# P.V of an attention kernel in eight tiles of the array instead of four, summed in two banks

## The chip, the cores and the metric

The kernel runs on one core of a Trainium2 chip. The metric is the device time of one execution in microseconds; smaller is better. The core's engines work side by side, each on its own queue: TensorE (PE, with its weight loads shown apart as PEld), VectorE (DVE), ScalarE (ACT), GpSimd (POOL) and SyncE (SP, which here only starts DMAs).

## The reference

The input is `x` of 2048 tokens by 512. It is normalised by layer, goes into a softmax attention over 32 heads of 16 dimensions (no mask) and, beside it, into a feed-forward network with a squared ReLU; the attention's result is multiplied by a SiLU gate made of the network's result and added to `x`. All is fp32.

```python
xn = layernorm(x)
q, k, v = split_heads(xn @ wqkv)                # 32 heads, 2048 x 16 each
p = softmax(einsum("bhqd,bhkd->bhqk", q, k) * 16 ** -0.5)
s = merge_heads(einsum("bhqk,bhkd->bhqd", p, v)) @ wo
h = relu(xn @ w1 + b1) ** 2                     # 2048 x 1792
out = x + s * silu(h @ w2 + b2)
```

## The kernel before

Three stages follow each other. The first normalises and transposes `x` and makes keys, queries and values, which go to HBM. The second, nearly all of the time, is 64 turns. The third sums up the last turn and writes the last rows.

A turn is eight of 512 steps. A step `(qd, qc, kb)` takes four heads (`qd`), 512 queries (`qc`) and 128 keys (`kb`). `scores` makes its P transposed, keys on the partitions and queries along the free side, for two heads at a time, in two matmuls on 64 rows of the array each. `exps` takes the exponential of 128 x 1024 numbers on ACT into a tile `P` in SBUF. V has a column of ones beside each head, so that the sums of the softmax come out of the same product.

Three kinds of work of PE share a turn, all in tiles of 64 rows by 128 columns, so that two matmuls in the two row halves can run side by side. The order is a string written out by hand, a letter for a slot:

- `S`: the scores of two heads into one of two PSUM buffers `S` of two banks, from which ACT takes the exponential at once (`scores`, `exps`, L299 and L303).
- `L`: one matmul in each row half for the feed-forward network, or late in the kernel for the output projection (`lin`, L347). They accumulate in the two banks `spare`. `/` ends the first half of such a block: the two halves change banks, behind a small instruction on POOL (`swap`, L373).
- `0`, `1`, `B`: the scores of one head aside (`aside`), by row half 0 into the bank `acc` (`sides[0]`), by row half 1 into the bank `lin` (`sides[1]`), or both. DVE copies the bank into the tile `P` in SBUF (L322), and ACT takes its exponential from there later. Beside a `0` or `1` stands an `L` of the other row half. Five pairs of such scores go this way in an ordinary turn, eleven through `S`.
- `E` ends one block and begins the next.

57 turns use the string `ORDINARY`, the first `FIRST`, four `TWO_PAIRS` and two `SHORT`.

At the end of a turn stands P.V for its eight steps (`values`, L572). V is the stationary side, 128 keys by 32 columns for a head (16 of them the head's values, the next the ones), and each head writes 32 partitions of the bank `acc`: four column tiles with all 128 rows. The products of eight steps accumulate there. Then `finish` takes the bank into the SBUF tile `ou`: in even turns with a copy (L583), in odd ones with an add of the turn before (L586), whose result goes to HBM. The tiny instructions of `see` follow: ACT and DVE each read an element of the last `P`, and DVE one of `sides[1]`. PE is free to write a side again when DVE has read it.

The lines of `fast_path` behind the turns add up the last turn in two halves of the columns (L884), and matmuls (L889) read the result.

Of the kernel before, what the change touches and what calls it, by code (L numbers as in the profile page):

```python
# [28 lines left out]
OP = mybir.AluOpType  # L29
# [18 lines left out]
@with_exitstack  # L48
def mha_ffn_kernel(ctx: ExitStack, tc: tile.TileContext, x, wqkv, wo, bx, w1, b1, w2, b2, out):
    nc = tc.nc  # L50
    x, out = x[0], out[0]
    ctx.enter_context(tc.manual_schedule())
    keep = ctx.enter_context(tc.tile_pool(name="keep", bufs=1))
    dram = ctx.enter_context(tc.tile_pool(name="dram", bufs=1, space=DRAM))

    ident = keep.tile([128, 128], FT, name="ident")
    make_identity(nc, ident)
    nvalid = keep.tile([1, 1], I32, name="nvalid")
    stat = keep.tile([128, 80], FT, name="stat")

    kdram = [[dram.tile([128, 2, 1024], FT, name=f"kd{g}_{h}") for h in range(2)] for g in range(4)]
    qdram = [[dram.tile([128, 2, 512], FT, name=f"qd{g}_{c}") for c in range(NC)] for g in range(4)]
    vdram = dram.tile([NK, 128, VW], FT, name="vd")
    xdram = [dram.tile([128, 2, 4, 512], FT, name=f"xd{c}") for c in range(3)]

    udram = [[dram.tile([2, 2, 16, 4, 512], FT, name=f"ud{g}_{c}") for c in range(NC)] for g in range(4)]
    zdram = [[dram.tile([4, 512], FT, name=f"zd{q}_{c}") for c in range(NC)] for q in range(NQ)]
    gdram = dram.tile([S, D], FT, name="gd")

    with tc.tile_pool(name="sb", bufs=1) as sb, tc.tile_pool(name="ps", bufs=1, space=PSUM) as ps:  # L70
        fast_path(tc, sb, ps, locals())
    general_path(tc, dram, nvalid, ident, vdram, kdram, qdram, gdram, x, wo, out)


def fast_path(tc, sb, ps, env):
# [6 lines left out]
    mm = nc.tensor.matmul  # L82
    dve, act, pool, sp = nc.vector, nc.scalar, nc.gpsimd, nc.sync
# [3 lines left out]
    def t(shape, dt, tag):  # L87

        cnt[0] += 1
        p = ps if tag in ("S", "lin", "acc") else sb  # L90
        if tag in BUFS:
            turn[tag] = turn.get(tag, -1) + 1
            n = turn[tag] % BUFS[tag]
            tag = f"{tag}{places[n] if tag == 'S' else n}"
        return p.tile(shape, dt, tag=tag, name=f"{tag}_{cnt[0]}")
# [190 lines left out]
    vq = {}  # L286
# [6 lines left out]
    ptile = {}  # L293
# [275 lines left out]
    def values(i):  # L569
        qd, qc, kb = steps[i]  # L570
        for j in (1, 2, 3, 0) if i % 2 else (0, 1, 2, 3):
            mm(sides[0][32 * j:32 * j + 32], vq[qd][:, kb, 17 * j:17 * j + 32], ptile[i, j // 2][:, j % 2],  # L572
               start=kb % 8 == 0, stop=kb % 8 == 7)

    part = [None]

    def finish(n):

        if n == TURNS - 1:
            return  # L580
        ou = t([128, 512], FT, "ou")
        if n % 2 == 0:
            dve.tensor_copy(ou, sides[0])  # L583
            part[0] = ou
            return
        dve.tensor_tensor(ou, sides[0], part[0], op=OP.add)  # L586
        qd, qc, _ = steps[8 * n]
        sp.dma_start(zdram[qd][qc], ou[16::32])
        for j in range(4):
            sp.dma_start(udram[qd // 2][qc][0, qd % 2, :, j], ou[32 * j:32 * j + 16])  # L590
        events.setdefault(2 * n + 2, []).insert(0, (load_sums, (qd, qc)))
        events.setdefault(2 * n + 3, []).insert(0, (rowsums, (qd, qc)))
# [188 lines left out]
    sides = [t([128, 512], FT, "acc"), t([128, 512], FT, "lin")]  # L781
# [20 lines left out]

    ORDINARY = "SLLSBLLLSLL0SL1LSLL/SBLLSLL0SL1LSLL0L1SLS"
    TWO_PAIRS = "SLLLLBLLS/SL0LL1SLLSSEBLLLSLLLS/BLLSLL0LS1S"

    SHORT = "SLLBSLSLL01SL0LS1S/0L1SL0SL1LL0SL1S"
# [2 lines left out]
    for n in range(TURNS):  # L811
        i = 8 * n
# [9 lines left out]
        later, aside_at = [], [0, 0]  # L822
        for row in TWO_PAIRS if makes else SHORT if short else ORDINARY if n else FIRST:
            if row == "S":
# [45 lines left out]
        for j in range(8):  # L870
            values(i + j)
        finish(n)
    for time in sorted(events):
        happen(time / 2)


    ou = t([128, 512], FT, "P0")
    zc, r = t([128, 16], FT, "zc"), t([128, 16], FT, "rc")
# [3 lines left out]
    half = [slice(0, 256), slice(256, 512)]  # L882
    for s in half:
        dve.tensor_tensor(ou[:, s], sides[0][:, s], part[0][:, s], op=OP.add)  # L884
    small = t([128, 2, 512], FT, "S")
    lins = [small[:, 1], t([128, 512], FT, "lin"), t([128, 512], FT, "acc"), two[:, 0]]
    rest(2, spare[:, 0])
# [6 lines left out]
    for i in range(4):  # L894
        for j in range(4):
            mm(small[32 * j:32 * j + 32, 0, cut[i]], r[:, 4 * i + j:4 * i + j + 1].broadcast_to([128, 32]), ident,  # L896
               start=True, stop=True)
# [19 lines left out]
    for j in range(2):  # L917
        for todo in ((0, 0), (0, 1)), ((1, 0),):
            for i in (2 * j, 2 * j + 1):
                group(lins[i], lambda p: (h, l)[p][:, cut[i]], lambda p: wlast[0][:, p],  # L920
                      start=len(todo) == 2, stop=len(todo) == 1, todo=todo)
# [123 lines left out]
```

## Time and profile before

| | |
|---|---|
| time, median of 2 runs | 1227.38 us (1226.91 and 1227.84) |
| span of the profiled execution, first to last instruction | 1225.5 us |
| mean granted clock of TensorE | 0.997 |
| PE busy | 1212.2 us, 99% |
| ACT busy | 1011.3 us, 83% |
| DVE busy | 813.5 us, 66% |
| POOL busy | 279.3 us, 23% |
| DMA moved | 147.30 MB, mean 120 GB/s |

The profiled execution has no time of its own beside its span; the two times lie 1.4 and 2.3 us above the span, in which the start and the end outside the instructions are not contained. A group of instructions is told as line, engine, operation, output and inputs, shape and count, then the busy time, the mean of one in ns and the engine's idle time ahead of it. A line of the timeline begins with the start and the length in us. The length of a matmul holds its way through the array, so that matmuls overlap: what counts is from start to start.

### The profile page before, as it was taken

The numbers are of one execution on the slowest core, as the hardware profiler recorded it, in microseconds if no ns is written. First come the engines' busy times: TensorE is split into PE (matmuls) and PEld (weight loads), VectorE is DVE, ScalarE is ACT, GpSimd is POOL, SyncE is SP. The second block draws the span as 40 slices with busy tenths as digits, with TensorE's granted clock in tenths as the row PEclk, the third lists the DMA queues.
The fourth block names the chain that finished last, engine by engine and source line by source line (L and its number), as shares of the span: only waits on it lengthen the run. The fifth ranks groups of instructions, "written<-read, shape, count | busy, mean of one in ns | idle before, by whom it ended". The sixth has DMA issues, their size and how long they took to land.

```text
span 1225.5 us, 24037 instructions
## 1 busy us (share of the span) xinstructions
PE 1212.2 (99%) x9925; PEld 715.8 (58%) x9925; DVE 813.5 (66%) x1297; ACT 1011.3 (83%) x1172; POOL 279.3 (23%) x223
## 2 busy tenths in 40 slices
PE   9999999999999999999999999999999999999996
PEld 8888755555555555555555555555555555555553
DVE  5542277676767775757686666676765758787776
ACT  4222489988889998888998888899998899899883
POOL 5000032122221220404022222230230403222212
PEclk9999999999999999999999999999999999999998
DMA  8675823232161323223423214141422232364445
GB/s 318 246 269 193 267 76 112 67 96 62 55 193 51 98 68 100 79 78 115 146 66 109 62 58 122 37 172 41 135 79 79 77 98 79 113 217 155 145 152 125
DMA packets 103878, 147.30 MB, mean 120 GB/s; under 512 B 42954, under 2 KB 57304, under 8 KB 102228
## 3 DMA queue, kind: packets, MB, share of 16 engines
q1 hardware_dynamic: 100612, 136.28, 34.6%
q0 software_dynamic: 2720, 8.65, 2.5%
q8 instruction: 79, 1.29, 0.4%
q10 hardware_dynamic: 432, 0.79, 0.2%
q14 instruction: 35, 0.29, 0.1%
HBM read 99.68 MB, written 46.00 MB: 119 GB/s over the span
## 4 chain that ended last, share of the span: by engine, by line
PE 98%; ACT 1%; DVE 0%; issue 0%; POOL 0%; DVEq 0%; POOLq 0%; ACTq 0%
PE acc L572 37%; PE spare L347 28%; PE S L299 14%; PE S L112 10%; PE acc L299 5%; PE lin L299 2%; ACT P L303 1%; PE lin L476 1%; PE S L213 1%; PE acc L112 0%; PE lin L112 0%; PE S L704 0%; PE acc L704 0%; DVE P L931 0%; DVE P L924 0%; PE S L896 0%
## 5 line engine op out<-in xcount | busy, mean ns | idle before, releaser
L303 ACT ACTIVATE P<-S 128x1024 f32<-128x1024 f32 x702 | 662.5, 1035 | 91.4 <-PE S L299 91.0
L572 PE MATMUL acc<-P,V 128*32 128x512 f32 x4096 | 452.7, 594 | 0.0
L322 DVE COPY P<-acc 128x512 f32<-128x512 f32 x322 | 222.7, 692 | 141.2 <-PE lin L299 75.8
L303 ACT ACTIVATE P<-P 128x1024 f32<-128x1024 f32 x322 | 314.5, 1083 | 0.0
L572 PEld LDWEIGHTS acc<-P,V 128*32 128x32 f32 x4096 | 126.6, 110 | 287.9 <-issue 267.8
L299 PE MATMUL S<-QA,KA 64*128 64x512 f32 x1404 | 289.8, 403 | 1.7 <-ACT P L303 1.7
L322 DVE COPY P<-lin 128x512 f32<-128x512 f32 x322 | 220.7, 685 | 1.2
L299 PEld LDWEIGHTS S<-QA,KA 64*128 64x128 f32 x1404 | 133.4, 184 | 110.4 <-issue 42.6
L105 POOL TENSOR_TENSOR wf1l<-wr,wf1h 128x1024 fp32r<-128x1024 f32 x28 | 68.4, 2443 | 291.6 <-ACT wf1h L99 112.0
L299 PE MATMUL lin<-QA,KA 64*128 64x512 f32 x322 | 127.2, 395 | 0.0
L299 PE MATMUL acc<-QA,KA 64*128 64x512 f32 x322 | 127.1, 395 | 0.0
L347 PE MATMUL spare<-xl,wf1h 64*128 64x512 f32 x464 | 96.9, 391 | 0.0
L373 POOL MEMSET note<- 1x1 f32 x68 | 6.0, 88 | 397.2 <-PE spare L347 387.6
L347 PE MATMUL spare<-xh,wf1l 64*128 64x512 f32 x480 | 92.8, 392 | 0.0
L105 POOL TENSOR_TENSOR hl<-T,hh 128x1024 fp32r<-128x1024 f32 x28 | 80.1, 2860 | 53.0 <-DVE hh L101 53.0
L347 PE MATMUL spare<-wf2l,hh 64*128 64x512 f32 x448 | 90.9, 390 | 0.0
L105 POOL TENSOR_TENSOR wf2l<-wr,wf2h 128x1024 fp32r<-128x1024 f32 x28 | 67.1, 2396 | 90.3 <-DVE wf2h L101 90.3
L586 DVE TENSOR_TENSOR ou<-acc,ou 128x512 f32<-128x512 f32 x31 | 21.4, 692 | 97.4 <-PE acc L572 91.5
L347 PE MATMUL spare<-wf2h,hl 64*128 64x512 f32 x448 | 83.4, 390 | 0.0
L347 PE MATMUL spare<-xh,wf1h 64*128 64x512 f32 x480 | 77.5, 392 | 0.0
L347 PE MATMUL spare<-wf2h,hh 64*128 64x512 f32 x448 | 71.7, 392 | 0.0
L583 DVE COPY ou<-acc 128x512 f32<-128x512 f32 x32 | 22.1, 692 | 70.5 <-PE acc L572 70.1
(239 smaller groups left out, 1332.7 us busy)
## 6 DMA issues: line engine op xcount, KB each, us to landing
wr<-in_B_w_dram SPq DMA_DIRECT2D x56, 512.0 KB
KA<-kd SPq DMA_DIRECT2D x64, 256.0 KB
QA<-qd SPq DMA_DIRECT2D x128, 128.0 KB
kd<-P SPq DMA_DIRECT2D x15, 512.0 KB
qd<-P SPq DMA_DIRECT2D x15, 512.0 KB
u<-ud SPq DMA_DIRECT2D x15, 512.0 KB
V<-vd SPq DMA_DIRECT2D x8, 664.0 KB
vd<-P SPq DMA_DIRECT2D x16, 280.0 KB
```

The source lines that it names most:

```text
L105: leng.tensor_tensor(lo, src, hi.bitcast(FT), op=OP.subtract)
L112: mm(dst, lhs(a, k), rhs(b, k), start=n == 0, stop=n == len(todo) - 1)
L213: nc.tensor.transpose(pt[:, k, 128 * j:128 * j + 128], xnorm[c, i][:, j, 128 * k:128 * k + 128], ident)
L299: mm(dst, k[r, p, 128 * (kb % 8):128 * (kb % 8) + 128], q[r, p], start=True, stop=True)
L303: act.activation(ptile[i, p], src, AF.Exp, scale=SCALE)
L322: dve.tensor_copy(ptile[i, p][:, hp], sides[hp])
L347: ins = mm(bank, self.lhs(a, k)[r], self.rhs(b, k)[r], start=n == 0 and self.at[other] == 0, stop=n == len(self.todo[half]) - 1 and self.a ...
L373: f = pool.memset(note[:, notes[0]:notes[0] + 1], 0.0)
L476: mm(idle[:, :128], ident, ident, start=True, stop=True)
L572: mm(sides[0][32 * j:32 * j + 32], vq[qd][:, kb, 17 * j:17 * j + 32], ptile[i, j // 2][:, j % 2], start=kb % 8 == 0, stop=kb % 8 == 7)
L583: dve.tensor_copy(ou, sides[0])
L586: dve.tensor_tensor(ou, sides[0], part[0], op=OP.add)
```

## The change

`values` splits each product of a head by rows: keys 0 to 63 go by the upper row half into `sides[0]`, keys 64 to 127 by the lower into `sides[1]`, each in a tile of 64 rows by 32 columns. `finish` adds the second bank on DVE, and so does the last sum. `ORDINARY` is another string with the same number of scores of each kind (one `B` has become a `0` and a `1`). `FIRST`, `TWO_PAIRS` and `SHORT` stay as they are.

```diff
     def values(i):
         qd, qc, kb = steps[i]
         for j in (1, 2, 3, 0) if i % 2 else (0, 1, 2, 3):
-            mm(sides[0][32 * j:32 * j + 32], vq[qd][:, kb, 17 * j:17 * j + 32], ptile[i, j // 2][:, j % 2],
-               start=kb % 8 == 0, stop=kb % 8 == 7)
+            for half in range(2):
+                r = slice(64 * half, 64 * half + 64)
+                mm(sides[half][32 * j:32 * j + 32], vq[qd][r, kb, 17 * j:17 * j + 32], ptile[i, j // 2][r, j % 2],
+                   start=kb % 8 == 0, stop=kb % 8 == 7)
...
         if n % 2 == 0:
             dve.tensor_copy(ou, sides[0])
+            dve.tensor_tensor(ou, sides[1], ou, op=OP.add)
             part[0] = ou
             return
         dve.tensor_tensor(ou, sides[0], part[0], op=OP.add)
+        dve.tensor_tensor(ou, sides[1], ou, op=OP.add)
...
-    ORDINARY = "SLLSBLLLSLL0SL1LSLL/SBLLSLL0SL1LSLL0L1SLS"
+    ORDINARY = "SLLS0L1LLS0LS1LLLS/BSLLLS0L1SLL0SL1LSLLS"
     TWO_PAIRS = "SLLLLBLLS/SL0LL1SLLSSEBLLLSLLLS/BLLSLL0LS1S"
     SHORT = "SLLBSLSLL01SL0LS1S/0L1SL0SL1LL0SL1S"
     FIRST = "SLLSLLBLSLL0SL1LSLL/SBLLSLL0SL1LSLL0L1SLS"
...
     for s in half:
         dve.tensor_tensor(ou[:, s], sides[0][:, s], part[0][:, s], op=OP.add)
+    for s in half:
+        dve.tensor_tensor(ou[:, s], sides[1][:, s], ou[:, s], op=OP.add)
```

## The prediction

> **What bounds the kernel now.** I read the page first (engines, chain, costliest groups).
>
> ```profile
> span 1225.5 us, 24037 instructions
> PE 1212.2 (99%) x9925; PEld 715.8 (58%) x9925; DVE 813.5 (66%) x1297; ACT 1011.3 (83%) x1172; POOL 279.3 (23%) x223
> PE 98%; ACT 1%; DVE 0%; issue 0%; POOL 0%; DVEq 0%; POOLq 0%; ACTq 0%
> L572 PE MATMUL acc<-P,V 128*32 128x512 f32 x4096 | 452.7, 594 | 0.0
> L572 PEld LDWEIGHTS acc<-P,V 128*32 128x32 f32 x4096 | 126.6, 110 | 287.9 <-issue 267.8
> L586 DVE TENSOR_TENSOR ou<-acc,ou 128x512 f32<-128x512 f32 x31 | 21.4, 692 | 97.4 <-PE acc L572 91.5
> ```
>
> PE sets the end: it carries 98% of the chain that ended last. The 512 steps of P.V have 2048 matmuls and 4096 records, since each fp32 matmul is two records. Next I cut the span into turns, from one P.V's start to the next, in the windows view.
>
> ```profile
> 257.45:264.46 7.00, 7.00 (x66) 1.98 (x65) 6.42 (x10) 6.01 (x8) 4.07 (x2) 1.00 0.26 80
> 257.45:273.98 16.53, 16.53 (x146) 9.30 (x145) 13.50 (x22) 14.98 (x18) 8.26 (x4) 1.00 0.47 144
> 174.03:191.43 17.39, 16.98 (x146) 9.03 (x145) 13.08 (x19) 15.02 (x18) 4.95 (x4) 1.00 0.15 40
> 1068.93:1085.04 16.11, 16.11 (x134) 8.07 (x133) 12.59 (x21) 15.35 (x18) 4.34 (x5) 1.00 0.49 171
> ```
>
> The columns behind the length are the busy time of PE, PEld, DVE, ACT and POOL. An ordinary turn takes 16.53 us, 7.00 of them P.V, with PE busy throughout. ACT is busy for 14.98 of the 16.53 us, so it is nearly as full. Of the 64 turns one runs FIRST, four TWO_PAIRS (the third window), two SHORT (the fourth), and 57 ORDINARY. Only ORDINARY gets another order. The timeline from one P.V to the next aside shows what the change touches.
>
> ```profile
> 263.92 0.61 PE L572 MATMUL acc<-P,V 128*32 128x512 f32 x4
> 264.46 0.19 PEld L299 LDWEIGHTS S<-QA,KA 64*128 64x128 f32 x2 [0.84 <-issue]
> 264.46 0.50 PE L299 MATMUL S<-QA,KA 64*128 64x512 f32 x2
> 264.60 0.69 DVE L583 COPY ou<-acc 128x512 f32<-128x512 f32 x1 [0.66 <-PE acc L572]
> 264.80 0.62 PE L347 MATMUL spare<-xh,wf1h 64*128 64x512 f32 x4
> 265.21 0.13 DVE L800 TENSOR_TENSOR seen<-P,lin 1x1 f32<-1x1 f32 x1
> 265.26 0.40 PE L299 MATMUL S<-QA,KA 64*128 64x512 f32 x2
> 265.35 0.18 PEld L299 LDWEIGHTS acc<-QA,KA 64*128 64x128 f32 x1
> 265.40 0.18 PEld L299 LDWEIGHTS lin<-QA,KA 64*128 64x128 f32 x1
> 265.50 0.39 PE L299 MATMUL acc<-QA,KA 64*128 64x512 f32 x1
> 265.96 0.40 PE L347 MATMUL spare<-xh,wf1h 64*128 64x512 f32 x2
> ```
>
> A pair of matmuls, one in each row half, takes a slot of 0.23 us (265.26 to 265.50). DVE empties acc from 264.60 to 265.29, and `see` ends at 265.34. The aside's weights for acc load at 265.35, 0.06 behind the copy, and those for lin at 265.40, 0.06 behind `see`, which reads lin. Both are early enough for the slot at 265.50. When the weights are not there ahead of time, as at 264.46, the next pair comes 0.34 instead of 0.23 us later: a late load costs 0.11 beside its lateness.
>
> **The change part by part.** *P.V itself.* Four tiles of 128 rows become eight of 64, with twice the matmuls and twice the weight loads.
>
> ```profile
> 257.13 0.39 PE L299 MATMUL S<-QA,KA 64*128 64x512 f32 x2
> 257.45 0.16 PEld L572 LDWEIGHTS acc<-P,V 128*32 128x32 f32 x8 [0.31 <-DVE P L322]
> 257.91 0.13 PEld L572 LDWEIGHTS acc<-P,V 128*32 128x32 f32 x4 [0.30 <-issue]
> 258.34 0.13 PEld L572 LDWEIGHTS acc<-P,V 128*32 128x32 f32 x4 [0.30 <-issue]
> ...
> 1210.32 1.08 PE L896 MATMUL S<-ident,rc 128*32 128x128 f32 x32
> 1211.22 0.19 PE L905 MATMUL spare<-ones,okm 128*1 128x1 f32 x2
> ```
>
> Records come in groups of four, one for each column tile, and a group takes 0.43 us (257.91 to 258.34). Sixteen groups are 6.9 of the 7.00 us. If the eight new tiles run side by side, a group holds eight records, there are still sixteen groups, and P.V's length stays. The pairs at L299 show that two row halves run side by side, the column tiles here that four columns do; no row shows both at once. Each record then has 0.43 / 8 = 54 ns of issue. PE has been seen to issue 32 such pairs of load and matmul between 1210.32 and 1211.22, 28 ns each; over a whole P.V it is seen at 0.43 / 4 = 107 ns. So the cost is bounded by nothing at 28 ns, and by 128 records x 107 ns = 13.7 us, 6.8 more in each turn, at 107. I take nothing: L896 is the row nearest in kind (fp32 in tiles of 32 columns, each record a quarter as long), though its 32 pairs are few beside the 128 of a P.V. The tiles of a group start one behind the other: four loads of 110 ns take 0.13 us together, so 0.02 us for three steps. Four more tiles make the last one 0.03 us later, once in a turn, since the groups overlap otherwise.
>
> *The switch of tile form.* From the last S pair to P.V are 0.32 us (257.13 to 257.45) where a slot is 0.23; from the last group to the next S are 264.46 - 263.92 = 0.54 where a group is 0.43, and the first S pair lacks early weights, another 0.11. Together with 0.02 in the first group (257.45 to 257.91 is 0.46) that is 0.34 us in each turn. Before and after, the columns go from 128 to 32 and back; the rows no longer change. The last turn shows a switch of columns alone.
>
> ```profile
> 1200.25 0.40 PE L704 MATMUL S<-xl,hl 128*128 128x512 f32 x1
> 1200.49 0.40 PE L704 MATMUL S<-xh,hl 128*128 128x512 f32 x1
> 1200.82 0.64 PE L572 MATMUL acc<-P,V 128*32 128x512 f32 x4
> ```
>
> It costs the same: 0.33 us behind 128*128 where its slot is 0.24. So I leave the 0.34 us as they are; the other end is a gain of 0.34 x 64 = 21.8 us. The Trainium skill ("TensorEngine Tiling (Array Packing)", Key Properties) says that a change of tiling mode drains the engine, and lists 64x128 and 64x32 as modes of their own; by it nothing is gained here either, and no run here shows that pair of forms.
>
> *The second add.* The new order starts a turn with S, L, L, S, aside 0, L, aside 1. DVE copies acc and then adds lin into the same `ou`. The copy has 264.60 to 265.29. An instruction that needs its forerunner's result starts behind its end:
>
> ```profile
> 276.23 2.21 DVE L424 TENSOR_TENSOR T<-T 128x1024 f32<-128x1024 f32 x1
> 278.48 0.69 DVE L101 CAST hh<-T 128x1024 fp32r<-128x1024 f32 x1
> ```
>
> That is 0.04 us (278.44 to 278.48). The add takes 0.69 (L586), so it has 265.33 to 266.02; `see` is next, starts 0.61 behind its forerunner's start as today (264.60 to 265.21), and ends at 266.07; lin's weights load from 266.13. Aside 1 stands two slots behind aside 0, where the trace has 265.96. Loaded late, it counts from 266.13 + 0.11 = 266.24: 0.28 us late. Queued behind it are all matmuls of the turn, since PE waits in order; aside 0 at 265.50 needs acc alone and is not delayed. The lower bound is 0.05: if the add starts 0.61 behind the copy's start, as instructions without such a need do, `see` ends at 265.95, the load starts at 266.01, and if it then hides, that is 0.05 behind 265.96. The upper is 0.5, if the copy itself comes 0.2 late because eight tiles finish later than four. I take 0.28, since both of its waits have a row.
>
> *ACT behind it.* ACT takes its first nine S pairs without a pause, and the last S pair of the turn needs the buffer of the ninth.
>
> ```profile
> 265.00 8.41 ACT L303 ACTIVATE P<-S 128x1024 f32<-128x1024 f32 x9 [1.54 <-PE S L299]
> ...
> 266.43 0.40 PE L299 MATMUL S<-QA,KA 64*128 64x512 f32 x2
> ...
> 273.65 0.40 PE L299 MATMUL S<-QA,KA 64*128 64x512 f32 x2
> ```
>
> The third S pair, today just in time (266.43, ready 0.43 later at 266.86; ACT is free at 265.00 + 2 x 8.41 / 9 = 266.87), moves one row back and waits with the rest: 266.43 + 0.23 + 0.28 = 266.94. ACT pauses 0.50 us, its ninth ends at 273.91 instead of 273.41, the buffer is free at 273.96, and a late load makes that 274.07. The last S pair is due at 273.65 + 0.28 = 273.93: 0.13 more. With no pause it is 0, the lower bound; with all 0.50 passed on, 0.22 of it beyond the 0.28, the upper.
>
> In an ordinary turn that is 0.28 + 0.13 + 0.03 = 0.44 us, and for 57 of them 25.1 us.
>
> *The seven other turns and the end.*
>
> ```profile
> 1075.93 0.50 PE L299 MATMUL S<-QA,KA 64*128 64x512 f32 x2
> 1076.82 0.18 PEld L299 LDWEIGHTS acc<-QA,KA 64*128 64x128 f32 x1 [0.36 <-DVE seen L800]
> ...
> 191.30 0.69 DVE L322 COPY P<-lin 128x512 f32<-128x512 f32 x1
> 191.43 1.06 PE L572 MATMUL acc<-P,V 128*32 128x512 f32 x8
> ...
> 1208.04 0.76 DVE L884 TENSOR_TENSOR P<-acc,ou 128x256 f32<-128x256 f32 x2 [2.92 <-PE acc L572]
> ```
>
> SHORT, where both sides are needed in the fourth slot, already shows this wait: PEld waits for `seen`, 0.89 us behind the first S. With the add lin is free 266.13 - 264.46 = 1.67 behind it, so SHORT loses 1.67 - 0.94 (lin is 0.05 behind acc, as at 265.40) = 0.73. TWO_PAIRS needs both in the sixth slot, 0.34 + 4 x 0.23 = 1.26 behind the first S, and loses 1.67 + 0.11 - 1.26 = 0.52. Both end with aside 1 and one S pair. P.V now waits for lin's copy as well: in TWO_PAIRS to 191.99 + 0.06, 0.62 behind 191.43; I take the same for SHORT. FIRST has four rows behind its last aside 1 and no sum ahead of it: 0.3. The last sum has two more half adds, 0.76, which the next matmuls need. 4 x 1.14 + 2 x 1.35 + 0.3 + 0.76 + 7 x 0.03 = 8.5 us; at least 5, if the waits for ACT in TWO_PAIRS swallow part.
>
> No DMA, POOL or SP instruction is added; the stores of `ou` leave 0.73 us later, and what is queued behind them on SP (`load_sums`, and the next `load_qa`) is used half a turn later or more. DVE's 44 us of new work lie in a 66% busy engine and cost only where named.
>
> Sum: 25.1 + 8.5 = 33.6 us. The span is 1225.5, so 1259.1; the median lies 1.9 above the span (1227.38), so **1261 us**, 2.7% slower. With the bounds (0.05 + 0.03 = 0.08 to 0.5 + 0.22 + 0.03 = 0.75 in an ordinary turn, and 5 to 8.5) this case reaches from 1237 to 1279. A difference of 2%, 24.5 us, is about what can be told from no change here.
>
> **The rivals.**
>
> *The add is hidden.* Place: aside 1 in slot seven. It decides at lin being free by 265.73 on the trace's scale, a slot ahead of aside 1 so that its load hides; that is 0.40 us earlier than worked out. For it: the new order puts the first aside of lin two slots later than today, and DVE is idle before the copy (0.66 us), so nothing else delays it. Against: SHORT's wait above. Then 0.03 x 57 remains, and of the seven turns and the end 5: 1227.4 + 6.7 = 1234, not measurably slower.
>
> *The switch is cheap.* If 64*128 to 64*32 needs no drain, up to 21.8 us come back. But aside 1 still hangs on DVE, which counts from P.V's last product; PE only arrives earlier and waits longer. What is left is the 0.09 + 0.02 us ahead of P.V: 1261 - 64 x 0.11 = 1254. Only if the add is hidden too is it 1234 - 21.8 = 1212, faster by 1.2%. Against: the row of 1200.82.
>
> *Eight tiles don't run together*, or issue limits them. If two groups of four follow each other, P.V takes 6.9 us more in each turn: 1261 + 64 x 6.9 = 1703. For it: no row shows more than four records at a time; against: 28 ns at L896. The Trainium skill ("TensorE: Matmul & The Clock Gate", "Wait - 56ns, not 53.3ns?") gives about 62 ns for each matmul when hardware decode is off; by it P.V would take an estimated 128 x 62 ns = 7.9 us, some 60 us more in all, and the rows at 1210.32, at 28 ns, speak against it as far as 32 matmuls go.
>
> **How the numbers follow.** The sum's case 0.61; the add hidden 0.15; the switch cheap 0.12; tiles not together 0.12. Within the first, 0.48 lie above 2% (1252) and 0.13 below; the second is within 2%; the third holds 0.09 within 2% and 0.03 faster, which needs P.V itself to be shorter in the new form as well, for which no row speaks; the fourth is slower. Slower 0.60, within 2% 0.37, faster 0.03. The range goes from 1232, just under the hidden add, to 1285, just over the sum's upper end; it leaves out the fourth case and the lower part of the third.
>
> **What would show it.** Right: P.V still 7.0 us with groups of eight every 0.43; PEld's wait for `seen` before lin's weights in each turn, about 0.3 us; the last S pair waiting for ACT; ordinary turns of 16.9 to 17.0 us. Wrong: P.V clearly shorter or longer than 7.0, the first S less than 0.1 behind P.V's end, or turns still at 16.5.

## The result, and the profile after

The changed kernel takes 1267.93 us (1267.80 and 1268.06) against 1227.38: 1.033 times as long, 95% interval 1.030 to 1.036. The profiled execution has a span of 1266.0 us at a granted clock of 0.998, 40.5 us above that of before. The page of the profile after has this (engines, chain, two of the costliest groups):

```profile
span 1266.0 us, 32359 instructions
PE 1245.5 (98%) x14021; PEld 742.7 (59%) x14021; DVE 855.8 (68%) x1362; ACT 1016.3 (80%) x1172; POOL 279.1 (22%) x223
PE 90%; DVE 7%; ACT 1%; issue 1%; DVEq 0%; POOL 0%; POOLq 0%; ACTq 0%
L574 PE MATMUL acc<-P,V 64*32 64x512 f32 x4096 | 457.8, 591 | 0.0
L574 PE MATMUL lin<-P,V 64*32 64x512 f32 x4096 | 453.9, 591 | 0.0
```

PE is busy for 98% of a longer span, but it no longer carries 98% of the chain that ended last: DVE has taken 7% of it, where it had 0%. The two groups at L574 are twice the 4096 records of before.

The windows view, with the columns as before, shows one P.V, an ordinary turn, a `TWO_PAIRS` turn, the turn behind it, and the first `SHORT` turn:

```profile
279.41:286.44 7.03, 7.03 (x130) 2.36 (x129) 4.29 (x5) 6.08 (x8) 4.78 (x2) 1.00 0.26 77
279.41:296.49 17.08, 16.99 (x210) 9.78 (x208) 12.50 (x19) 15.05 (x18) 4.87 (x3) 1.00 0.15 41
175.44:193.46 18.02, 17.50 (x210) 9.53 (x209) 12.94 (x19) 15.10 (x18) 4.94 (x4) 1.00 0.16 39
193.46:211.15 17.69, 17.59 (x211) 10.71 (x209) 12.07 (x22) 15.11 (x18) 5.19 (x3) 1.00 0.49 158
1103.10:1119.91 16.81, 16.45 (x198) 8.50 (x196) 12.83 (x21) 15.31 (x18) 4.35 (x5) 1.00 0.48 162
```

P.V has about twice the records in the same time, 7.03 us against 7.00. The ordinary turn has grown from 16.53 to 17.08; the median from one P.V's start to the next is 16.51 before and 17.07 after, 0.56 more. The growth lies outside P.V. The timeline shows where, from the last tile of P.V to the first aside of `lin`, and at the end of the turn:

```profile
285.87 0.59 PE L574 MATMUL acc<-P,V 64*32 64x512 f32 x1
...
285.92 0.59 PE L574 MATMUL lin<-P,V 64*32 64x512 f32 x1
286.44 0.50 PE L299 MATMUL S<-QA,KA 64*128 64x512 f32 x2
286.61 0.69 DVE L589 TENSOR_TENSOR ou<-acc,ou 128x512 f32<-128x512 f32 x1 [2.85 <-PE lin L574]
287.41 0.69 DVE L590 TENSOR_TENSOR ou<-lin,ou 128x512 f32<-128x512 f32 x1
287.48 0.39 PE L299 MATMUL acc<-QA,KA 64*128 64x512 f32 x1
288.02 0.13 DVE L804 TENSOR_TENSOR seen<-P,lin 1x1 f32<-1x1 f32 x1
288.20 0.18 PEld L299 LDWEIGHTS lin<-QA,KA 64*128 64x128 f32 x1 [0.53 <-DVE seen L804]
288.20 0.49 PE L299 MATMUL lin<-QA,KA 64*128 64x512 f32 x1
288.54 0.64 PE L347 MATMUL spare<-wf2l,hh 64*128 64x512 f32 x4
...
289.46 6.54 ACT L303 ACTIVATE P<-S 128x1024 f32<-128x1024 f32 x7 [0.54 <-PE S L299]
...
295.54 0.63 PE L347 MATMUL spare<-wf2h,hl 64*128 64x512 f32 x4
296.06 0.19 PEld L299 LDWEIGHTS S<-QA,KA 64*128 64x128 f32 x2 [0.32 <-ACT P L303]
296.49 0.10 PEld L574 LDWEIGHTS acc<-P,V 64*32 64x32 f32 x1 [0.25 <-issue]
```

Aside 1 stands two slots behind aside 0 (287.48), so it was due at 287.94. It waits for `see`, that for the second add, that for the first, and starts at 288.20: 0.26 late. The next pair comes 0.34 behind it rather than 0.23, so 0.37 in all. At the end of the turn the last S pair waits for ACT, which has paused 0.54 us for the third S pair and ends the ninth at 296.00 (289.46 + 6.54). Two slots of `L` begin at 295.54, so the pair was due at 296.01 and loads at 296.06; P.V follows 0.43 behind it, where it was 0.32 behind a pair with early weights. That is 0.05 + 0.11 = 0.16. With the 0.03 of P.V the two waits make 0.56.

The view of waits has the same two places. Its columns are the sum, the count and the longest. Of after:

```profile
ACT P L303 <- PE S L299: 126.2, 126, 2.1
PEld S L299 <- ACT P L303: 34.7, 136, 0.8
PEld lin L299 <- DVE seen L804: 34.2, 63, 0.7
```

And of before:

```profile
ACT P L303 <- PE S L299: 91.0, 66, 1.6
PEld S L299 <- ACT P L303: 19.0, 92, 0.8
```

The wait for `seen` comes 63 times, in every turn but the first, and was not among the waits of `lin` before. The first row counts ACT's pauses, which cost PE nothing by themselves; the second is where PE waits in turn.

### The profile page after: what moved, and what is told of

Its sections match the earlier page's. It is cut to its first block, busy times and chain, and to the rows that moved or that the text cites. A ratio compares the mean times of both kernels' runs of the same rounds, so it can differ in the third digit from the quotient of the medians.

```text
span 1266.0 us, 32359 instructions
## 1 busy us (share of the span) xinstructions
PE 1245.5 (98%) x14021; PEld 742.7 (59%) x14021; DVE 855.8 (68%) x1362; ACT 1016.3 (80%) x1172; POOL 279.1 (22%) x223
## 3 DMA queue, kind: packets, MB, share of 16 engines
q0 software_dynamic: 2720, 8.65, 2.5%
## 4 chain that ended last, share of the span: by engine, by line
PE 90%; DVE 7%; ACT 1%; issue 1%; DVEq 0%; POOL 0%; POOLq 0%; ACTq 0%
PE acc L574 32%; PE spare L347 23%; PE S L299 11%; PE S L112 10%; PE lin L299 5%; PE lin L574 4%; PE acc L299 2%; DVE ou L586 2%; DVE ou L590 2%; DVE ou L585 2%; DVE ou L589 2%; ACT P L303 1%; PE lin L476 1%; PE S L213 0%; PE acc L112 0%
## 5 line engine op out<-in xcount | busy, mean ns | idle before, releaser
L574 PE MATMUL acc<-P,V 64*32 64x512 f32 x4096 | 457.8, 591 | 0.0
L574 PE MATMUL lin<-P,V 64*32 64x512 f32 x4096 | 453.9, 591 | 0.0
L299 PE MATMUL S<-QA,KA 64*128 64x512 f32 x1404 | 296.0, 412 | 1.7 <-ACT P L303 1.7
L574 PEld LDWEIGHTS acc<-P,V 64*32 64x32 f32 x4096 | 151.9, 107 | 243.4 <-issue 237.0
L574 PEld LDWEIGHTS lin<-P,V 64*32 64x32 f32 x4096 | 143.7, 107 | 14.0 <-issue 8.6
L299 PE MATMUL lin<-QA,KA 64*128 64x512 f32 x322 | 133.3, 414 | 7.1 <-DVE seen L804 0.7
L347 PE MATMUL spare<-xl,wf1h 64*128 64x512 f32 x464 | 104.6, 392 | 0.0
L347 PE MATMUL spare<-xh,wf1h 64*128 64x512 f32 x480 | 97.5, 399 | 0.0
L347 PE MATMUL spare<-wf2h,hh 64*128 64x512 f32 x448 | 89.4, 400 | 0.0
L299 PEld LDWEIGHTS lin<-QA,KA 64*128 64x128 f32 x322 | 59.1, 184 | 48.5 <-DVE seen L804 34.2
```

The source lines that it names most:

```text
L299: mm(dst, k[r, p, 128 * (kb % 8):128 * (kb % 8) + 128], q[r, p], start=True, stop=True)
L347: ins = mm(bank, self.lhs(a, k)[r], self.rhs(b, k)[r], start=n == 0 and self.at[other] == 0, stop=n == len(self.todo[half]) - 1 and self.a ...
L574: mm(sides[half][32 * j:32 * j + 32], vq[qd][r, kb, 17 * j:17 * j + 32], ptile[i, j // 2][r, j % 2], start=kb % 8 == 0, stop=kb % 8 == 7)
```

## The experiments

The theory: three waits, each 57 to 64 times. The second add holds `lin` (0.37), the new order alone makes the last S pair wait for ACT (0.16), and eight tiles start 0.03 later than four. The rivals put the loss into the tiles themselves (issue, or a dearer switch of form) or into the order of slots. In the first four experiments the theory's time lies within 2.5 us of the measured one and every rival's at least 8 us away; the theory's prices were read from the profile after. In the comparisons of the first four the kernel before took 1226.8 us.

**The order alone, in the kernel before.**

```diff
 (before)
-    ORDINARY = "SLLSBLLLSLL0SL1LSLL/SBLLSLL0SL1LSLL0L1SLS"
+    ORDINARY = "SLLS0L1LLS0LS1LLLS/BSLLLS0L1SLL0SL1LSLLS"
```

> The kernel before with the new ORDINARY alone, P.V in four tiles of 128 rows into one bank. Theory (the added time is three waits: aside 1 for the second add, 0.37 us in an ordinary turn, the last S pair for ACT, 0.17, and 0.02 for eight tiles): the wait for ACT is the order's own, so it stays. Ordinary turns 16.51 + 0.19 = 16.70 us, 57 x 0.19 = 10.8, so 1238 us. Rival one (the order costs nothing by itself, all of it hangs on the add): 1227, turns of 16.51. Rival two (the tile form costs, not the waits): also 1227.

Measured: 1235.57 us (1235.31 to 1236.42), 1.007 [1.006, 1.009] of before. Its ordinary turn in the windows view:

```profile
475.89:492.56 16.67, 16.67 (x147) 9.28 (x145) 8.79 (x14) 15.06 (x18) 0.09 (x1) 1.00 0.05 10
```

ACT's first nine S pairs and the end of that turn in its timeline:

```profile
483.43 8.65 ACT L303 ACTIVATE P<-S 128x1024 f32<-128x1024 f32 x9 [1.46 <-PE S L299]
...
491.61 0.64 PE L347 MATMUL spare<-xh,wf1l 64*128 64x512 f32 x4
492.13 0.19 PEld L299 LDWEIGHTS S<-QA,KA 64*128 64x128 f32 x2 [0.31 <-ACT P L303]
492.56 0.16 PEld L572 LDWEIGHTS acc<-P,V 128*32 128x32 f32 x8 [0.24 <-issue]
```

ACT takes 8.65 us for nine pairs where the kernel before took 8.41. The end of the turn looks as in the changed kernel: the last S pair 0.05 late, P.V 0.43 behind it. (The 0.02 for eight tiles in the expectation has no place in a kernel with four.) So the order costs 0.16 in an ordinary turn by itself, without a second bank and without an add, 8.8 us in all.

**No second add.** The keys 64 to 127 of each block are left out of the sums; all else is the changed kernel.

```diff
             dve.tensor_copy(ou, sides[0])
-            dve.tensor_tensor(ou, sides[1], ou, op=OP.add)
...
         dve.tensor_tensor(ou, sides[0], part[0], op=OP.add)
-        dve.tensor_tensor(ou, sides[1], ou, op=OP.add)
...
-    for s in half:
-        dve.tensor_tensor(ou[:, s], sides[1][:, s], ou[:, s], op=OP.add)
```

> The changed kernel without the adds of the second bank, so the products of the lower 64 keys of each block are left out of the sums; P.V still writes both banks. Theory: aside 1 no longer waits, the wait for ACT and the P.V waits for lin's copy at the end of TWO_PAIRS, SHORT and FIRST stay: ordinary turns 16.51 + 0.02 + 0.19 = 16.72, and 12 + 4 = 16 us in all, 1243. Rival one (the order costs nothing): 1233. Rival two (the eight tiles themselves, or the switch to them, cost): stays near 1268.

Measured: 1241.51 us (1240.86 to 1242.64), 1.012 [1.011, 1.014]. Its windows for P.V, an ordinary turn and the turn behind `TWO_PAIRS`:

```profile
477.16:484.19 7.03, 7.03 (x130) 2.35 (x128) 0.97 (x1) 6.07 (x8) 0.00 (x0) 1.00 0.01 2
477.16:493.84 16.68, 16.68 (x210) 9.56 (x208) 8.79 (x15) 15.04 (x18) 0.09 (x1) 1.00 0.04 10
191.55:208.84 17.29, 17.29 (x211) 10.89 (x209) 11.36 (x21) 15.08 (x18) 5.18 (x3) 1.00 0.52 162
```

The add is worth 1267.9 - 1241.5 = 26.4 us. What stays above the order alone, 5.9 us, is the second bank: 64 x 0.03, and 0.6 in each of the six P.V that follow `TWO_PAIRS` and `SHORT` (17.29 against 16.68), where P.V waits for the copy of `lin`; the P.V behind `FIRST` waits 0.3. Eight tiles instead of four cost nothing more.

**Another order for the changed kernel**, with the first aside of `lin` four slots behind that of `acc` instead of two.

```diff
 (after)
-    ORDINARY = "SLLS0L1LLS0LS1LLLS/BSLLLS0L1SLL0SL1LSLLS"
+    ORDINARY = "SLLS0LLS1LL0SL1SLL/SBLLSLL0SL1LS0LL1SLLS"
```

> The changed kernel with a third ORDINARY, in which aside 1 stands a slot later, the third S pair a slot earlier, and the last aside 1 well ahead of P.V: SLLS0LLS1LL0SL1SLL/SBLLSLL0SL1LS0LL1SLLS. Both adds stay. Theory: lin is free 1.76 us behind the first S and the first aside of lin is due 1.97 behind it, so that all three waits vanish: ordinary turns 16.51 + 0.02 = 16.53; what is left are the seven other turns and the end, 57 x 0.02 + 5.0 + 2.5 + 0.3 + 0.8 = 10 us, 1237. Rival two (the tile form or the 44 us of DVE work cost by themselves, wherever they stand): turns of 17.0, 1265 or so.

Measured: 1238.60 us (1238.06 to 1238.91), 1.009 [1.008, 1.011]. Its ordinary turn in the windows view:

```profile
476.01:492.55 16.54, 16.54 (x211) 9.41 (x209) 9.36 (x15) 14.95 (x18) 0.09 (x1) 1.00 0.04 10
```

The loads of `lin` in its view of groups (after the bar: busy time, mean, idle time and its releasers):

```profile
L299 PEld LDWEIGHTS lin<-QA,KA 64*128 64x128 f32 x322 | 59.1, 184 | 11.9 <-DVE seen L804 3.5 <-DVE P L322 0.5
```

The add still runs in every turn, and all of its 0.37 is gone from the ordinary ones; `seen` holds `lin` for 3.5 us in all, not 34.2. With ACT's wait gone too, 16.54 is within 0.03 of before. The cost was a matter of when, not of DVE's work. This order moves several slots at once, so it doesn't part the two waits; the two experiments before do.

**The order of before in the changed kernel.**

```diff
 (after)
-    ORDINARY = "SLLS0L1LLS0LS1LLLS/BSLLLS0L1SLL0SL1LSLLS"
+    ORDINARY = "SLLSBLLLSLL0SL1LSLL/SBLLSLL0SL1LSLL0L1SLS"
```

> The changed kernel with the old ORDINARY, in which both sides are needed in the fifth slot. Theory: the wait for lin grows to 1.76 + 0.11 - 1.04 = 0.83 us, and the last aside 1 makes P.V wait another 0.3: ordinary turns 16.51 + 0.02 + 1.13 = 17.66, 57 x 1.15 + 9 = 75 us, 1302. Rival one (the new order was the loss): 1238 or less. Rival two (the tile form): 1268 as with the new order.

Measured: 1304.37 us (1302.83 to 1306.40), 1.063 [1.061, 1.065]. From its view of waits:

```profile
PEld lin L299 <- DVE seen L804: 41.1, 63, 0.7
```

The start of a P.V in its timeline:

```profile
514.34 0.61 PE L574 MATMUL acc<-P,V 64*32 64x512 f32 x1
514.68 0.61 PE L574 MATMUL lin<-P,V 64*32 64x512 f32 x1
```

The `B` in the fifth place needs `lin` two slots earlier, 0.46 more to wait for than in the changed kernel (PEld's 41.1 us are the part that is idle), and P.V's second tile waits 0.34 for the copy of the last aside. The new order is a mend for the two banks: by itself it costs 8.8 us, and with two banks the kernel is 36.4 us faster with it than with the order of before.

**Which tiles stand next to each other.** Two kernels ask why eight tiles run together: in the first the four heads of a step go by one row half and then by the other; in the second all eight steps go by the upper half first.

```diff
 (after, values)
-        for j in (1, 2, 3, 0) if i % 2 else (0, 1, 2, 3):
-            for half in range(2):
+        for half in range(2):
+            for j in (1, 2, 3, 0) if i % 2 else (0, 1, 2, 3):
```

> The changed kernel, with the four heads of a step first in the upper row half and then in the lower, instead of half by half for each head. Theory (a tile waits for its own rows and columns alone, so eight still run together): P.V 7.0 us, groups of eight records every 0.43, 1268 us. Rival (eight run together only because the two halves of a head stand next to each other in the program): PE takes four at a time, P.V up to 6.9 us longer in each of 64 turns, up to 1268 + 442 = 1710 us.

Measured: 1262.21 us in one run, before 1226.29 beside it. The rival falls: P.V has its 7.03 us. That it is 5.7 us below the changed kernel was not expected; 1.1 of it the kernel before shows as well in that session. Its timeline between two turns:

```profile
489.20 0.61 PE L574 MATMUL lin<-P,V 64*32 64x512 f32 x4
489.74 0.50 PE L299 MATMUL S<-QA,KA 64*128 64x512 f32 x2
489.86 0.69 DVE L589 TENSOR_TENSOR ou<-acc,ou 128x512 f32<-128x512 f32 x1 [6.19 <-PE lin L574]
490.65 0.69 DVE L590 TENSOR_TENSOR ou<-lin,ou 128x512 f32<-128x512 f32 x1
491.45 0.18 PEld L299 LDWEIGHTS lin<-QA,KA 64*128 64x128 f32 x1 [0.48 <-DVE seen L804]
```

Its ordinary turn in the windows view:

```profile
482.71:499.72 17.01, 16.97 (x210) 9.58 (x208) 9.48 (x16) 15.05 (x18) 0.09 (x1) 1.00 0.04 10
```

DVE begins 0.12 behind the first S instead of 0.17, `lin` loads 1.71 behind it instead of 1.76, and the turn is 0.06 shorter. What the chain through DVE gives, the turn gives: a small dose of the same cause. Most of the rest comes from the turns behind `TWO_PAIRS` and `SHORT`, where the upper half now ends 0.6 us before the lower. They took 17.25 to 17.28 us behind `TWO_PAIRS`, where the changed kernel has 17.69. As this is one run, its total is good to a few tenths of a per cent at best.

In the second kernel `values` takes the halves that it is to do as a second argument.

```diff
 (after, end of a turn)
-        for j in range(8):
-            values(i + j)
+        for half in range(2):
+            for j in range(8):
+                values(i + j, (half,))
```

> The changed kernel, with all eight steps of the upper row half first and then all eight of the lower: 64 records of one half stand ahead of the first of the other. Theory as far as the traces of before and after bear it out (PE starts records of free tiles out of the program's order, by some eight records at least): if it looks 64 records ahead, P.V stays at 7.0 us and the time at 1268; if it looks ahead by a group or two only, the halves follow each other, P.V is about 13.9 us and the time 1268 + 64 x 6.9 = 1710 us. I expect the second. Rival (order inside P.V doesn't matter): 1268.

Measured: 1569.73 us in one run, before 1226.29. P.V and the turn in its windows view:

```profile
574.62:586.83 12.21, 12.21 (x131) 3.63 (x129) 1.63 (x2) 6.22 (x8) 0.00 (x0) 1.00 0.01 1
574.62:596.48 21.86, 21.86 (x210) 11.05 (x208) 9.47 (x16) 15.18 (x18) 0.09 (x1) 1.00 0.03 8
```

The matmuls of P.V in its timeline where one half hands over to the other, and DVE's first add:

```profile
578.51 1.90 PE L574 MATMUL acc<-P,V 64*32 64x512 f32 x16
579.83 0.63 PE L574 MATMUL lin<-P,V 64*32 64x512 f32 x4
580.22 0.61 PE L574 MATMUL acc<-P,V 64*32 64x512 f32 x4
580.28 0.61 PE L574 MATMUL lin<-P,V 64*32 64x512 f32 x4
580.65 0.61 PE L574 MATMUL acc<-P,V 64*32 64x512 f32 x4
580.71 0.61 PE L574 MATMUL lin<-P,V 64*32 64x512 f32 x4
581.08 0.61 PE L574 MATMUL acc<-P,V 64*32 64x512 f32 x4
581.14 1.90 PE L574 MATMUL lin<-P,V 64*32 64x512 f32 x16
...
581.76 0.69 DVE L589 TENSOR_TENSOR ou<-acc,ou 128x512 f32<-128x512 f32 x1 [6.21 <-PE acc L574]
```

Neither the expected 1710 nor the rival's 1268 came out. The order in the program does matter, but PE starts the first records of the lower half at 579.83 with 12 of the upper half still to come (three groups of four, from 580.22 on); so it is in 63 of the 64 turns, with 8 in the other. Four groups of each half overlap, so P.V is 12 groups longer, 12 x 0.43 = 5.2, and not 16. The turn grows by 4.79 only: the first add now runs during P.V, and `lin` is free when its aside is due, which gives the 0.37 back.

## Why the prediction was right or wrong

Slower was the likeliest, 1261 us, and the range 1232 to 1285 holds the 1267.9. Step by step:

- *P.V keeps its length, plus 0.03.* Right: 7.03. The cost of issue was taken at nothing, on one short row, between bounds 6.8 us apart, and 128 records fit into 7.03 us, 55 ns each. The kernel with the halves by step shows it again.
- *The switch of tile form stays at 0.34 us.* Right: 0.52 us from P.V's last tile to the first S (285.92 to 286.44), the same as before when counted from the last tile. From the last S pair to P.V the kernel with the other order, whose last pair has its weights early, has 0.33 (492.22 to 492.55), where the prediction read 0.32. The Trainium skill's rule ("TensorEngine Tiling (Array Packing)", Key Properties) that a change of mode drains agrees with these 0.52 us: 64 rows on both sides don't spare it.
- *The second add holds aside 1 for 0.28.* The mechanism was right and the term too small: 0.37. The load of `lin` was put 1.67 behind the first S and came at 1.76. Of these 0.09, 0.03 is DVE's first instruction (0.17 behind the first S, before 0.14). These are not the 0.03 of P.V a second time, since the first S stands 0.52 behind the last tile in both. The kernel without the second add has 0.17 too, and the one with the halves by step 0.12, so they go with the tiles and their order; why was not tried. 0.06 is the gap between the adds: 287.30 to 287.41 is 0.10, where I took 0.04 from a pair of DVE instructions on SBUF alone. The row was of the right kind by its dependence and not by its waits: the second add waits for PE too, though P.V is long done. The wait for the forerunner is then a record of its own, which the view of the chain shows:

```profile
287.34 0.02 DVEq L590
```

It starts 0.04 behind the forerunner's end, and the add 0.07 behind it. That the second bank lies in PSUM is not needed for this: in the kernel before, L195, which works on SBUF alone, starts 0.04 behind L190 where it has one wait, and 0.11 behind it in the two places (28.9 and 37.2 us) where such a record stands between. So the price was to be had before the run. The bounds, 0.05 and 0.5, held it.
- *ACT behind it, 0.13.* Measured 0.16. The working tied it to the third S pair moving back one row. The order alone has the pause of ACT and the same 0.16, and the other order, whose third S pair stands a slot earlier than before, has neither; the third pair was not moved by itself. The price was slightly low (by the prediction's own figures, 274.07 against 273.93, it is 0.14).
- *The seven other turns and the end, 8.5.* 40.5 - 57 x 0.56 = 8.6. In the rows: `TWO_PAIRS` 18.02 against 17.39, 0.63 for my 0.52; the P.V behind it 0.62 as worked out; the first `SHORT` turn 16.81 against 16.11, 0.70 for my 0.73. In the 8.6 are also 0.6 by which the first P.V starts later (158.10 against 157.51), which no term has, so that the agreement to 0.1 is in part luck.

So the miss of 6.9 us lies in one place: an ordinary turn loses 0.56 and not 0.44, and 57 x 0.12 = 6.8. Three quarters of that is the second add's wait. The rivals fell: the add is not hidden (26.4 us come back without it), a cheap switch would show as a first S nearer than 0.52 to P.V's last tile, and eight tiles do run together. The estimate worked out from the Trainium skill's 62 ns for each matmul with hardware decode off ("TensorE: Matmul & The Clock Gate", "Wait - 56ns, not 53.3ns?") did not hold here, at 55 ns.

The measured parts are order 8.8, second bank 5.9 and second add 26.4, together 41.1 us; they add up by construction, since each is one kernel less the kernel before it, and another sequence gives other parts: in the order of before, bank and add together cost 77.6. No version here beats the kernel before; the nearest one with both banks, the other order, is 0.9% above it.

## What to carry to other kernels

More and smaller tiles that fill the same array bought nothing here, where the groups stayed as many, and a second accumulation bank brought a second read, for which the next user of that bank waits: price that read by the first user of the bank, counted from the last product, with every gap in between. Where an order is written by hand, ask of each added wait whether the slot that meets it can stand later; here another order was worth 29 us with the same work, as it met both this wait and the one for ACT. Take the gap between two dependent instructions from a row with the same waits, not only the same dependence.

## What the runs showed of the hardware

- Matmuls in different tiles do not start in the program's order. With the halves by turn, records of the lower half start at 579.83, ahead of 12 records of the upper half that come first in the program. The Trainium skill ("TensorE: Matmul & The Clock Gate", "The mechanism") says that matmuls start and end strictly in the program's order; this run shows otherwise, and the measurement decides. A wait was not passed, though: behind aside 1 of the changed kernel, which waits for `see` until 288.20, stands an `L` for the other row half, and it starts at 288.21 and not before.
- That reach has an end: 12 records here, three groups. Until then the tiles of the lower half stand idle; that cost 5.2 us in a P.V of 7.0.
- Eight tiles of 64 rows by 32 columns start about 7 ns apart (285.87 to 285.92), and a group of eight takes the same 0.43 us as a group of four with 128 rows.
- A DVE instruction that waits for its forerunner and for another engine started 0.10 us behind the forerunner's end (L590; 0.11 at L195), with a record of its own for the first wait; one that waits for its forerunner alone 0.04.
